# A retention block and two MLPs: the first two loads of weights behind the fourth unit's inputs, and loads planned at 390 bytes a ns

## The chip, the cores and the metric

The kernel runs on one core of a Trainium2 chip. The metric is the device time of one execution in microseconds (us). The kernel before has a median of 909.39 us over 3 runs (909.02 to 910.09). The engines are named as in the profile: PE is TensorE (matmuls), PEld its loads of weights, DVE VectorE, ACT ScalarE, POOL GpSimd, SP SyncE, which issues nearly all DMAs.

## The reference

```python
# retention: 4 batches, 8 heads, 576 positions, 64 dims
scores = (1 / sqrt(64)) * q @ k^T
gamma  = 1 - 2 ** (-5 - head)
ret    = scores * where(i >= j, gamma ** (i - j), 0)
x = (ret @ v)  as [2304 tokens, 512]
# first MLP: w_in 512 x 2048, w_out 2048 x 512
h = maximum(x @ w_in, 0);  x = (h * h) @ w_out
# second MLP: w_a, w_b 512 x 1536, w_out 1536 x 512
return ((x @ w_a) * (x @ w_b)) @ w_out
```

All inputs but q, k and v, which are 32-bit floats, are weights in 64-bit floats.

## The kernel before

**One planner orders everything.** The kernel doesn't issue its instructions as it goes. Each piece of work is a step, added to a list with the engine it uses, its estimated cost and what it depends on (`Plan.add`). `Plan.order` then simulates the engines: working back from the end it gives each step a due time, and going forward it takes, on the engine that is free next, the step that is due first among those that are ready. The result is a fixed order for each engine, and on the chip each engine works through its own strictly in that order. The planner knows loads and stores by the bytes that they move: `dmac` (line 244) costs a transfer of n bytes at n / 260 ns, at least 620 ns. All such transfers go through one queue, issued by SyncE (line 242), again in the planned order.

**Attention** is done in 20 units: for each of 4 batches four pairs of heads over the first 7 chunks of 64 positions, and one unit for the two chunks left of all pairs. A unit loads its queries and keys (tile `qkr`, three buffers) and its values and keys (tile `vr`, three buffers), scales the latter by decays on ScalarE (line 475, tile `tv`), multiplies scores, states and sums on TensorE, masks the scores on VectorE (line 565, tile `pt`), carries states (lines 586 and 587) and writes its product to `xt`, the MLP's input (line 550). The first four units are the head pairs of batch 0. With three buffers, the fourth unit's `qkr` takes the buffer that the first unit has used.

**Weights** come as 64-bit floats, 512 KB for a tile of 128 x 512, into raw buffers (`wraw`: four of their own and two lent from the part of `xt` that is filled last, shown as `xt_68`). `w_load` (lines 321 to 382) turns a raw tile into 32-bit form with integer steps: the magnitude of the high words on ScalarE (line 342, tile `wf`), a clamp, a shift and a sign on VectorE (346, 353, 361), the low words on ScalarE (368, tile `we`) and their addition on VectorE (372). The sum is then split: ScalarE casts its high half into a slot `w` (line 377, shown as the helper's line 233), and VectorE subtracts that from the sum for the low half (line 380, shown as 236). Inputs of the MLPs are split in the same way (`split_x`: a cast at 233 and a subtraction at 236 for each of four tiles `x` of a block of tokens). Each product is then three matmuls: high by high, low by high, high by low.

**The MLPs** run over groups of chunks of the hidden width, each group over five blocks of tokens. The first group (8 chunks of the first MLP) is interleaved with attention: block t is planned when `READY[t]` parts of attention are (two parts to a batch: its four pairs, and its unit for the rest). Weights are loaded in the order of use (`pump`, `todo`), first into 16 slots. When attention is finished, `enter` (line 759) gives its buffers free and puts in their place `yt`, three raw buffers (`raw`) and three further weight slots; a group's result that was stored to memory before that (tile `y`, through `r`) is loaded back into `yt`.

The planner's `extra` argument adds dependencies by hand. Every step's dependencies, also those, hold in the planner's simulation; on the chip, a load waits only for the buffers and data it needs and for its place in SyncE's order. `env` is a small dictionary that attention and the MLPs share.

Of the kernel before, what the change touches and what calls it, by code (L numbers as in the profile page):

```python
# [13 lines left out]
U32 = mybir.dt.uint32  # L14
# [9 lines left out]
NP = H // 2  # L24
# [172 lines left out]
def act(n, psum=False):  # L197
    return 0.833 * n + (110 if psum else 140)

def dve(n):  # L200
    return 1.042 * n + 70

def dve2(n):
    return 0.521 * n + 190

def pool(n):
    return 2.3 * n + 150

@with_exitstack
def tile_retention_two_mlps(  # L210
# [13 lines left out]
    plan = Plan()  # L224
# [7 lines left out]
    def copy(o, i):  # L232
        return lambda e: A.copy(o(), i()) if e == "ACT" else eng[e].tensor_copy(o(), i())  # L233

    def sub(o, a, b):
        return lambda e: eng[e].tensor_sub(o(), a(), b())  # L236
# [4 lines left out]
    def dma(o, i):  # L241
        return lambda e: nc.sync.dma_start(out=o(), in_=i())

    def dmac(bytes_):
        return {"DMA": max(620.0, bytes_ / 260.0)}

    big = ctx.enter_context(tc.tile_pool(name="big", bufs=1))
    dram = ctx.enter_context(tc.tile_pool(name="dram", bufs=1, space=bass.MemoryType.DRAM))
# [10 lines left out]
    def slot(tag):  # L259
        r = rings[tag]  # L260
        i = r[1] % len(r[0])
        r[1] += 1
        plan.renew((tag, i))
        return r[0][i], (tag, i)
# [45 lines left out]
    def raw_slot():  # L310

        if state_["entered"] is None:
            raw, key = slot("wraw")
            return lambda: raw, key, []
        n = state_["loads"]
        state_["loads"] += 1
        key = ("late", n % RAWS)
        plan.renew(key)
        return lambda: raws[n % RAWS], key, [state_["entered"]]

    def w_load(ph, c, j, i):

        w, kw = slot("wf")
        rest, ke = slot("we")
        src = (w1 if ph == 1 else w2)[c, :, j, :]
        parts = [("w", i, 0), ("w", i, 1)]
        ex = [state_["entered"]] if i >= NW0 else []
        wu = w.bitcast(U32)

        raw, kraw, exr = raw_slot()  # L330
        def lo():
            return raw()[:, 0::2]

        def hi():
            return raw()[:, 1::2]

        plan.add(
            dmac(P * 4096),
            dma(raw, lambda: src.bitcast(U32)), w=[kraw], extra=exr,
        )  # L340
        plan.add(
            {"ACT": act(512)}, lambda e: A.activation(w, hi().bitcast(F32), AF.Abs), [kraw], [kw]  # L342
        )
        plan.add(
            {"DVE": dve2(512)},
            lambda e: V.tensor_scalar(  # L346
                out=w, in0=w, scalar1=F64_MIN, scalar2=F64_MAX, op0=ALU.max, op1=ALU.min
            ),
            w=[kw],
        )  # L350
        plan.add(
            {"DVE": dve2(512)},
            lambda e: V.tensor_scalar(  # L353
                out=wu, in0=wu, scalar1=3, scalar2=0x3FFFFFF8,
                op0=ALU.logical_shift_left, op1=ALU.bitwise_and,
            ),
            w=[kw],
        )
        plan.add(
            {"DVE": dve(512)},  # L360
            lambda e: V.scalar_tensor_tensor(  # L361
                out=wu, in0=hi(), scalar=0xC0000000, in1=wu, op0=ALU.bitwise_and, op1=ALU.bitwise_or
            ),
            [kraw], [kw],
        )
        plan.add(
            {"ACT": act(512)},
            lambda e: A.activation(rest, lo(), AF.Copy, scale=LO_ULPS), [kraw], [ke],  # L368
        )
        plan.add(  # L370
            {"DVE": dve(512)},
            lambda e: V._custom_dve(  # L372
                ADD32_U16LIMBS, out=w.bitcast(U16), in0=w.bitcast(U16), in1=rest.bitcast(U16)
            ),
            [ke], [kw],
        )
        plan.add({"ACT": act(512)}, copy(lambda: wslot[i][:, 0, :], lambda: w), [kw], parts[:1], ex)
        plan.add(
            {"DVE": dve(512), "POOL": pool(512)},
            sub(lambda: wslot[i][:, 1, :], lambda: w, lambda: wslot[i][:, 0, :]),  # L380
            [kw, parts[0]], parts[1:], ex,
        )

    def pump():
        while todo:
            i = state_["next"] % state_["n"]
            if i in used.values():
                return
            used[todo[0]] = i
            wt[todo[0]] = i  # L390
            state_["next"] = i + 1
            w_load(*todo.pop(0), i)
# [4 lines left out]
    def attention():  # L397
# [8 lines left out]
        for h in half:  # L406
# [7 lines left out]
                w=[("mask",)],  # L414
            )

        def decays(p):
            plan.add(
                {"DVE": 230},
                lambda e: V.tensor_scalar(  # L420
                    out=md[:, p], in0=mask, scalar1=vt[:, p:p + 1], scalar2=None, op0=ALU.mult
                ),
                [("mask",), ("vt",)], [("md", p)],
            )

        class Unit:
# [13 lines left out]
            def load(self):  # L440
                b, n, m = self.b, len(self.cells), len(self.leave)
                o = 2 * C * LONG * (NP if self.p is None else self.p)
                self.r, self.kr = slot("qkr")
                plan.add(
                    dmac(P * 8 * C * n),
                    dma(lambda: self.r[:, :2 * n * C], lambda: qk[b][:, o:o + 2 * n * C]), w=[self.kr],
                )
                if (b, self.p) == (0, 0):
                    plan.add(
                        {"ACT": 470}, lambda e: A.dma_start(out=vt, in_=vtab), w=[("vt",)], lag=2200  # L450
                    )

                    plan.add(
                        {"ACT": 1500}, lambda e: A.copy(first[:, 1:], first[:, :1]), [("first",)],
                        [("tv", 0)],
                    )
                self.v, self.kv = slot("vr")
                plan.add(
                    dmac(P * 4 * D * (n + m)),
                    dma(lambda: self.v[:, :(n + m) * D], lambda: vk[b][:, o:o + (n + m) * D]),  # L460
                    w=[self.kv],
                )
                if (b, self.p) == (0, 0):
                    plan.add(dmac(P * 4 * C * NP), dma(lambda: gt, lambda: gtab), w=[("gt",)])
                if b == 0 and self.p is not None:
                    decays(self.p)
                self.tv, self.kt = slot("tv")
                for q in self.pairs:
                    js = [i for i, x in enumerate(self.leave) if x[0] == q]
                    vs = [i for i, x in enumerate(self.cells) if x in self.leave and x[0] == q]  # L470
                    to = slice(js[0] * D, (js[-1] + 1) * D)
                    ti = slice(vs[0] * D, (vs[-1] + 1) * D)
                    plan.add(
                        {"ACT": 0.833 * len(js) * D + 250},
                        lambda e, to=to, ti=ti, q=q: A.activation(  # L475
                            self.tv[:, to], self.v[:, ti], AF.Copy, scale=vt[:, NP + q:NP + q + 1]
                        ),
                        [self.kv, ("vt",)], [self.kt],
                    )
# [131 lines left out]

    xs = {}
    y1 = {}
    env = {"done": 0}

    def split_x(gi, t):
        ph = GROUPS[gi][0]
# [269 lines left out]
```

## Time and profile before

| | |
|---|---|
| median of 3 runs | 909.39 us (909.02 to 910.09) |
| profiled execution | 911.62 us, its span 909.9 us |
| PE busy | 893.1 us (98% of the span), 6256 matmuls |
| DVE busy | 490.3 us (54%) |
| ACT busy | 383.2 us (42%) |
| data moved | 66.12 MB, 73 GB/s over the span |
| DMA share in the first six slices of 40 | 0.8, 0.7, 0.8, 0.3, 0.5, 0.3 |

The page divides the span into 40 slices of 22.7 us. TensorE's busy share is 0.6 in the first, 0.8 in the second and 0.9 or more in every other. The DMA engines are busy for the most part in the first three slices, in which attention's inputs and the first weights are loaded. VectorE's share is 0.9 or more in the second and the fourth slice. The trace holds 49 packets of the queue of instructions (q8, 0.80 MB): the engines' programs are themselves read from memory while the kernel runs.

### The profile page before, as it was taken

How to read it: one execution, taken by the hardware profiler on the slowest of the kernel's cores; microseconds unless marked ns; L12 is line 12 of the kernel's file. 1: busy time of each engine (PE TensorE's matmuls, PEld its weight loads, DVE VectorE, ACT ScalarE, POOL GpSimd, SP SyncE). 2: the span in 40 equal slices, each digit the busy share in tenths (PEclk: the TensorE clock that was granted, in tenths of full speed). 3: DMA queues.
4: the chain of work that ended last, by engine and by line, in shares of the span. 5: the costliest groups of instructions: out<-in, count | busy, mean ns of one | idle time of the engine just before them, and what ended most of it. 6: DMA issues, size and time to landing. Idle time of an engine off the chain costs nothing.

```text
span 909.9 us, 14978 instructions
## 1 busy us (share of the span) xinstructions
PE 893.1 (98%) x6256; PEld 755.6 (83%) x6256; DVE 490.3 (54%) x974; ACT 383.2 (42%) x707; POOL 0.7 (0%) x6
## 2 busy tenths in 40 slices
PE   6899999999999999999999999999999999999998
PEld 6787888788898889888888888898888888888888
DVE  6899545721599847965595223289332253323323
ACT  3676334653586435643364223266222132221221
POOL 0000000000000000000000000000000000000000
PEclk9999999999999999999999999999999999999999
DMA  8783532811043300320032000024000000011101
GB/s 276 276 278 124 171 117 71 278 58 58 24 123 110 116 1 24 96 67 1 0 98 89 1 1 1 1 82 142 8 1 1 1 1 1 2 45 47 43 5 70
DMA packets 22100, 66.12 MB, mean 73 GB/s; under 512 B 2448, under 2 KB 3088, under 8 KB 22032
## 3 DMA queue, kind: packets, MB, share of 16 engines
q1 hardware_dynamic: 21888, 65.15, 22.0%
q8 instruction: 49, 0.80, 0.4%
q14 instruction: 19, 0.16, 0.1%
q10 hardware_dynamic: 144, 0.01, 0.0%
HBM read 57.28 MB, written 7.86 MB: 72 GB/s over the span
## 4 chain that ended last, share of the span: by engine, by line
PE 93%; DVE 5%; DMA 1%; ACT 1%; issue 1%; DVEq 0%; ACTq 0%
PE bank L227 93%; DVE wf L372 1%; DVE wf L361 1%; DVE w L236 1%; DVE sa L587 1%; DMA y<-r 0%; DVE pt L565 0%; DMA vt<-vtab 0%; DVE xt L550 0%; DVE wf L346 0%; DVE wf L353 0%; DVE gh L236 0%; ACT r L697 0%; DVE xt L239 0%; ACT tv L475 0%
## 5 line engine op out<-in xcount | busy, mean ns | idle before, releaser
L227 PE MATMUL bank<-x,w 128*128 128x512 f32 (+1 forms) x2400 | 537.2, 369 | 3.4 <-ACT r L697 1.6
L227 PEld LDWEIGHTS bank<-x,w 128*128 128x128 f32 x2400 | 421.3, 189 | 80.8 <-ACT r L697 2.6
L227 PE MATMUL bank<-gh,w 128*128 128x512 f32 (+1 forms) x1680 | 387.1, 369 | 1.2 <-ACT r L233 0.8
L227 PEld LDWEIGHTS bank<-gh,w 128*128 128x128 f32 x1680 | 295.8, 188 | 55.2 <-ACT r L233 1.2
L697 ACT ACTIVATE r<-bank 128x512 f32<-128x512 f32 (+1 forms) x140 | 77.5, 553 | 313.5 <-PE bank L227 310.5
L706 DVE TENSOR_TENSOR g<-bank,r 128x512 f32<-128x512 f32 (+1 forms) x60 | 38.3, 638 | 180.3 <-PE bank L227 179.4
L236 DVE TENSOR_TENSOR gh<-g,gh 128x512 fp32r<-128x512 f32 (+1 forms) x140 | 88.9, 635 | 81.1 <-ACT g L711 56.1
L233 ACT CAST gh<-g 128x512 fp32r<-128x512 f32 (+1 forms) x100 | 57.7, 577 | 110.9 <-DVE g L706 94.8
L236 DVE TENSOR_TENSOR x<-yt,x 128x512 fp32r<-128x512 f32 (+1 forms) x60 | 36.0, 634 | 50.2 <-ACT x L233 50.1
L233 ACT CAST w<-wf 128x512 fp32r<-128x512 f32 x68 | 41.6, 616 | 23.2 <-DVE wf L372 20.6
L236 DVE TENSOR_TENSOR w<-wf,w 128x512 fp32r<-128x512 f32 x68 | 46.5, 686 | 8.8 <-ACT w L233 8.4
L372 DVE CUSTOM_DVE_ANT_0 wf<-wf,we 128x1024 uint16<-128x1024 uint16 x68 | 46.6, 686 | 1.1
L236 DVE TENSOR_TENSOR x<-xt,x 128x512 fp32r<-128x512 f32 (+1 forms) x60 | 37.2, 634 | 12.2 <-ACT x L233 9.2
L702 DVE SCALAR_TENSOR_TENSOR g<-bank,r 128x512 f32<-128x512 f32 (+1 forms) x40 | 25.4, 636 | 30.5 <-ACT r L697 30.2
L368 ACT ACTIVATE we<-raw 128x512 int32<-128x512 uint32 x52 | 34.6, 669 | 14.5 <-DVE wf L372 14.2
L233 ACT CAST x<-xt 128x512 fp32r<-128x512 f32 (+1 forms) x60 | 33.7, 575 | 16.4 <-PE bank L227 15.9
L342 ACT ACTIVATE wf<-raw 128x512 f32<-128x512 f32 x52 | 34.4, 671 | 4.2 <-DMA raw<-w 2.4
L361 DVE SCALAR_TENSOR_TENSOR wf<-raw,wf 128x512 uint32<-128x512 uint32 x52 | 35.3, 686 | 0.2
L233 ACT CAST x<-yt 128x512 fp32r<-128x512 f32 (+1 forms) x60 | 33.4, 576 | 4.9 <-PE bank L227 4.0
L346 DVE TENSOR_SCALAR wf<-wf 128x512 f32<-128x512 f32 x68 | 28.1, 421 | 5.2 <-ACT wf L342 4.6
L239 DVE TENSOR_TENSOR yt<-bank,yt 128x512 f32<-128x512 f32 (+1 forms) x40 | 23.3, 630 | 11.3 <-PE bank L227 11.3
L353 DVE TENSOR_SCALAR wf<-wf 128x512 uint32<-128x512 uint32 x68 | 28.1, 421 | 0.3
(42 smaller groups left out, 365.9 us busy)
## 6 DMA issues: line engine op xcount, KB each, us to landing
raw<-w SPq DMA_DIRECT2D x52, 512.0 KB, 3.7
vr<-vk SPq DMA_DIRECT2D x16, 448.0 KB, 4.6
qkr<-qk SPq DMA_DIRECT2D x16, 448.0 KB, 5.0
wraw<-w SPq DMA_DIRECT2D x12, 512.0 KB, 6.5
out<-xt SPq DMA_DIRECT2D x16, 256.0 KB, 2.1
y<-r SPq DMA_DIRECT2D x12, 256.0 KB, 3.0
yt<-y SPq DMA_DIRECT2D x3, 1024.0 KB, 8.4
qkr<-qk SPq DMA_DIRECT2D x4, 512.0 KB, 4.9
```

What stands on the lines that cost most here:

```text
L227: T.matmul(o, l, r, start=start, stop=stop, skip_group_check=True)
L233: return lambda e: A.copy(o(), i()) if e == "ACT" else eng[e].tensor_copy(o(), i())
L236: return lambda e: eng[e].tensor_sub(o(), a(), b())
L342: {"ACT": act(512)}, lambda e: A.activation(w, hi().bitcast(F32), AF.Abs), [kraw], [kw]
L346: lambda e: V.tensor_scalar(out=w, in0=w, scalar1=F64_MIN, scalar2=F64_MAX, op0=ALU.max, op1=ALU.min),
L353: lambda e: V.tensor_scalar(out=wu, in0=wu, scalar1=3, scalar2=0x3FFFFFF8, op0=ALU.logical_shift_left, op1=ALU.bitwise_and,),
L361: lambda e: V.scalar_tensor_tensor(out=wu, in0=hi(), scalar=0xC0000000, in1=wu, op0=ALU.bitwise_and, op1=ALU.bitwise_or),
L368: lambda e: A.activation(rest, lo(), AF.Copy, scale=LO_ULPS), [kraw], [ke],
L372: lambda e: V._custom_dve(ADD32_U16LIMBS, out=w.bitcast(U16), in0=w.bitcast(U16), in1=rest.bitcast(U16)),
L697: lambda e, o=o: A.activation(r[:, :n], o[:, :n], fn), [ko], [kr],
L702: V.scalar_tensor_tensor(out=g[:, :n], in0=o[:, :n], scalar=0.0, in1=r[:, :n], op0=ALU.max, op1=ALU.mult)
L706: V.tensor_mul(g[:, :n], o[:, :n], r[:, :n])
```

## The change

The planner's cost of a transfer goes from bytes / 260 to bytes / 390 ns. And while `env["hold"]` holds a step, every load of a raw weight gets it as a further dependency. The step is the load of queries and keys of the unit (0, NP - 1), the fourth unit; the number `len(plan.steps)` is the one that the load is about to get. Nothing sets `hold` back, so that it stands in the dependencies of the later loads of weights too, where it has long been fulfilled.

```diff
     def dmac(bytes_):
-        return {"DMA": max(620.0, bytes_ / 260.0)}
+        return {"DMA": max(620.0, bytes_ / 390.0)}
...
         plan.add(
             dmac(P * 4096),
-            dma(raw, lambda: src.bitcast(U32)), w=[kraw], extra=exr,
+            dma(raw, lambda: src.bitcast(U32)), w=[kraw], extra=exr + env["hold"],
         )
...
                 self.r, self.kr = slot("qkr")
+                if (b, self.p) == (0, NP - 1):
+                    env["hold"] = [len(plan.steps)]
                 plan.add(
                     dmac(P * 8 * C * n),
                     dma(lambda: self.r[:, :2 * n * C], lambda: qk[b][:, o:o + 2 * n * C]), w=[self.kr],
                 )
...
-    env = {"done": 0}
+
+    env = {"done": 0, "hold": []}
```

What this does to the order shows best at three places. The first is SyncE's queue at the start, as the difference of the two orders: `wraw` and `xt_68` are raw weights, `qkr` and `vr` the inputs of attention's units; the six loads of the first three units and the table `gt` stand ahead of this piece.

```order
-L242 DMA wraw_125<-w 128x1024
-L242 DMA wraw_127<-w 128x1024
 L242 DMA qkr_113<-qk 128x896
 L242 DMA vr_116<-vk 128x896
+L242 DMA wraw_125<-w 128x1024
 L242 DMA vr_117<-vk 128x768
 L242 DMA qkr_114<-qk 128x1024
-L242 DMA wraw_126<-w 128x1024
+L242 DMA wraw_127<-w 128x1024
 L242 DMA qkr_115<-qk 128x896
 L242 DMA vr_118<-vk 128x896
+L242 DMA wraw_126<-w 128x1024
```

The two weights that stood ahead of the fourth unit's `qkr_113` stand behind it now, the first one place after its `vr_116`, and the third weight moves two places back; `xt_68` follows in both orders, and in the new one `wraw_128` stands right behind it, where two loads of the seventh unit came first.

The second place is ScalarE and VectorE at the first block of the MLP, where `x_84` to `x_87` are the split halves of its inputs. On ScalarE, as the difference of the two orders:

```order
 L342 ACTIVATE wf_79<-wraw_126 128x512
 L368 ACTIVATE we_83<-wraw_126 128x512
-L475 ACTIVATE tv_120<-vr_118,vt 128x448
-L233 CAST w_95<-wf_79 128x512
+L342 ACTIVATE wf_78<-xt_68 128x512
+L342 ACTIVATE wf_81<-wraw_128 128x512
 L233 CAST x_84<-xt_65 128x512
 L233 CAST x_85<-xt_65 128x512
 L233 CAST x_86<-xt_65 128x512
 L233 CAST x_87<-xt_65 128x512
```

The conversions of the fourth and the fifth raw weight (`xt_68` and `wraw_128`) now stand ahead of the four casts of x; the scaling of the sixth unit's values and the cast of the third weight have moved behind them.

On VectorE before, at the same place, the four subtractions of x in their surroundings:

```order
L372 ISA wf_79<-wf_79,we_83 128x1024
L550 TENSOR_TENSOR xt_65<-bank_76,gt 128x4x64
L550 TENSOR_TENSOR xt_66<-bank_76,gt 128x4x64
L565 TENSOR_TENSOR pt_122<-bank_74,md 128x448
L236 TENSOR_TENSOR w_95<-wf_79,w_95 128x512
L236 TENSOR_TENSOR x_84<-xt_65,x_84 128x512
...
L236 TENSOR_TENSOR x_87<-xt_65,x_87 128x512
L586 COPY sa_124<-bank_75 128x64
```

And on VectorE in the changed order (its lines are two or three further down):

```order
L552 TENSOR_TENSOR xt_65<-bank_76,gt 128x4x64
...
L236 TENSOR_TENSOR x_84<-xt_65,x_84 128x512
...
L236 TENSOR_TENSOR x_87<-xt_65,x_87 128x512
L236 TENSOR_TENSOR w_96<-wf_80,w_96 128x512
L372 ISA wf_79<-wf_79,we_83 128x1024
...
L567 TENSOR_TENSOR pt_122<-bank_74,md 128x448
L236 TENSOR_TENSOR w_95<-wf_79,w_95 128x512
...
L552 TENSOR_TENSOR xt_66<-bank_76,gt 128x4x64
```

Five steps that came before the subtractions of x come behind them now: the subtractions for `w_95` and `w_96`, the addition for `wf_79`, the mask `pt_122` and the product into `xt_66`.

The third place is ScalarE at the change of phase (`enter`), where `raw` are the first weights after it and `r` the results that are emptied from the banks. Before:

```order
L233 COPY r_90<-bank_71 128x512
L342 ACTIVATE wf_78<-raw_2119 128x512
L368 ACTIVATE we_82<-raw_2119 128x512
L233 COPY r_91<-bank_72 128x512
L342 ACTIVATE wf_79<-raw_2120 128x512
L233 CAST w_2122<-wf_78 128x512
L233 COPY r_90<-bank_73 128x512
```

In the changed order:

```order
L233 COPY r_90<-bank_71 128x512
L342 ACTIVATE wf_78<-raw_2118 128x512
L368 ACTIVATE we_82<-raw_2118 128x512
L342 ACTIVATE wf_79<-raw_2119 128x512
L368 ACTIVATE we_83<-raw_2119 128x512
L342 ACTIVATE wf_80<-raw_2120 128x512
L233 COPY r_90<-bank_73 128x512
L233 CAST w_2121<-wf_78 128x512
```

The raw buffers' numbers are one lower. The copy out of `bank_72` has left ScalarE (it stands on VectorE now), and the conversion of the third raw weight stands ahead of the copy out of `bank_73`.

## Rows read from the trace of the kernel before

**Rows 1.** Timeline of TensorE, 12.5 to 17.1 us: start, busy, instructions [idle before <-releaser]

```profile
14.75 1.45 PE L227 MATMUL bank<-pt,vr 64*64 64x64 f32 x25 [1.88 <-issue]
...
16.97 0.36 PE L227 MATMUL bank<-qkr 64*64 64x64 f32 x1
```

**Rows 2.** Waits of TensorE: who waits <- for whom: us, times, longest

```profile
PE bank L227 <- DVE w L236: 0.4, 1, 0.4
```

**Rows 3.** Stretches: length, busy PE, PEld, DVE, ACT, POOL (instructions), clock, DMA share, GB/s

```profile
0.00:5.00 5.00, 0.00 (x0) 0.00 (x0) 0.44 (x4) 1.92 (x3) 0.67 (x6) 1.00 0.61 199
5.00:10.00 5.00, 4.72 (x122) 4.72 (x124) 3.16 (x12) 0.89 (x2) 0.00 (x0) 1.00 1.03 413
20.00:25.00 5.00, 3.83 (x126) 3.69 (x128) 4.96 (x16) 3.04 (x9) 0.00 (x0) 1.00 0.94 309
25.00:32.00 7.00, 4.87 (x130) 4.12 (x129) 6.83 (x15) 4.02 (x9) 0.00 (x0) 1.00 1.02 387
70.00:85.00 15.00, 15.00 (x275) 11.95 (x273) 15.00 (x37) 9.94 (x18) 0.00 (x0) 1.00 0.41 135
```

**Rows 4.** Timeline of VectorE around the first subtractions of x, and its last wait

```profile
29.11 0.75 DVE L550 TENSOR_TENSOR xt<-bank,gt 128x256 f32<-128x256 f32 x2
29.78 0.61 DVE L565 TENSOR_TENSOR pt<-bank,md 128x448 f32<-128x448 f32 x1
30.91 2.49 DVE L236 TENSOR_TENSOR x<-xt,x 128x512 fp32r<-128x512 f32 x4
...
57.31 0.69 DVE L236 TENSOR_TENSOR w<-wf,w 128x512 fp32r<-128x512 f32 x1 [0.56 <-ACT w L233]
```

**Rows 5.** Waits of VectorE, 32 to 58 us

```profile
DVE sa L586 <- PE bank L227: 1.4, 2, 0.9
DVE w L236 <- ACT w L233: 0.8, 2, 0.6
DVE wf L346 <- ACT wf L342: 0.8, 1, 0.8
DVE gh L236 <- ACT g L711: 0.4, 1, 0.4
```

**Rows 6.** Timeline of SyncE: the issue of some loads

```profile
0.80 0.38 SPq L242 DMA_DIRECT2D vr<-vk  x1
...
4.55 0.82 SPq L242 DMA_DIRECT2D wraw<-w  x2
11.45 0.33 SPq L242 DMA_DIRECT2D qkr<-qk  x1
...
17.62 0.33 SPq L242 DMA_DIRECT2D qkr<-qk  x1
```

**Rows 7.** DMA queues, 12.0 to 12.2 us, then 12.2 to 12.4: packets, MB, share

```profile
q1 hardware_dynamic: 18, 0.05, 63.5%
...
q8 instruction: 1, 0.02, 32.9%
q1 hardware_dynamic: 9, 0.01, 17.1%
```

**Rows 8.** Loads from issue to landing, 0 to 100 us: tile qkr, then tile w

```profile
DMA to landing us min/median/max: 3.9/5.2/9.8
...
DMA to landing us min/median/max: 4.4/6.8/11.0
```

**Rows 9.** Timeline of ScalarE: the first conversion of a weight, the first casts of x

```profile
11.81 0.67 ACT L342 ACTIVATE wf<-wraw 128x512 f32<-128x512 f32 x1 [1.03 <-DMA wraw<-w]
...
29.75 2.18 ACT L233 CAST x<-xt 128x512 fp32r<-128x512 f32 x4
```

**Rows 10.** Change of phase: SyncE's load of the third raw weight; TensorE's two waits

```profile
153.30 0.43 SPq L242 DMA_DIRECT2D raw<-w  x1
...
161.22 0.96 PE L227 MATMUL bank<-gh,w 128*128 128x512 f32 x3 [0.82 <-ACT r L233]
...
163.08 1.20 PE L227 MATMUL bank<-x,w 128*128 128x512 f32 x4 [0.90 <-ACT r L697]
```

## The prediction

> **What bounds the kernel now.** I read the busy shares first (TensorE has work over 893.1 of 909.9 us, on the page), then TensorE's waits, then the busy time by stretches, and last the queues of the first 90 us in order of time. TensorE's work is the same in both kernels, so only its stops count, 909.9 - 893.1 = 16.8 us, the wait for the first input and the tail behind the last matmul among them. What can move are the stops of the first 90 us and two at the change of phase near 161 us. At 12.9 us TensorE stands still for 1.88 us with "issue" as the reason, that is, for nothing that the profile shows as a wait [rows 1]. And at 85 us it waits for VectorE's low half of a weight [rows 2]. VectorE is busy 15.00 of 15.00 us from 70 to 85 [rows 3], and its last wait before that ends at 57.31 us [rows 4]; those between 32 and 58 us are four kinds, 3.4 us together [rows 5]. So from 57 to 85 us VectorE sets the pace, and TensorE arrives there as early as VectorE lets it. That is the yardstick for all that happens at the start: a lead of TensorE at 31 us is worth what VectorE can keep of it.
>
> **What the change does not do.** In the kernel before, the fourth unit's queries and keys leave SyncE at 11.45 us, long after the two weight loads at 4.55 [rows 6], because they need the buffer that the first unit's sums set free. In the changed order the same matmuls release them. The weights did not take their place in the queue; what they did was to fill the DMA engines up to 12.3 us.
>
> **Part 1, the stop at 12.9 us.** It falls inside one step (25 of its matmuls follow at 14.75 [rows 1]), so no operand is what it waits for. The queue of instruction packets handles its first packet in the window 12.2 to 12.4, just as the data queue falls from a share of 63.5% to 17.1% [rows 7]. By bytes: 0.995 MB in the first 5 us (5.00 x 199) and 413 GB/s after it [rows 3] put the end of the first seven loads (2.88 MB) at 9.6 us and of the two weights (3.93 MB) at 12.1. I read it so: the instructions waited behind the weights. Without these the packet can go at about 10, some 2.2 us sooner, and the stop of 1.88 us goes.
>
> The Trainium skill, DMA: Bandwidth & Descriptors, section "Queues, rings and completion order", says that each DMA engine serves its queues in turn, a packet at a time; an instruction packet would then wait for one packet of data and not for a megabyte. By that rule the stop is not the weights' doing, and it stays; the second rival gives the time of this case. The rows at 12.2 us speak against it, but they are one event.
>
> What is late next, once the stop is gone: the fourth unit's queries and keys. The shortest landing of such a load is 3.9 us [rows 8], which makes 15.35 for the scores that stood at 16.97 [rows 1]: 1.6 us earlier. The fifth unit's load is issued when the second unit's sums end; those took 2.9 us from 14.75 to 17.62 [rows 1, 6] and end by 15.8 when they go on at 12.9, so it is at least 1.8 us earlier at issue, though now behind a weight.
>
> **Part 2, the later weights.** The first weight leaves SyncE at about 12.3 instead of 4.55. What decides is ScalarE's order before the first x casts: it now converts two more raw weights there, the last of them the fifth load (wraw_128). From the fourth unit's queries and keys to that load SyncE issues eleven transfers: five weights of 0.524 MB, queries and keys of 0.459, 0.524 and 0.459, values and keys of 0.459, 0.393 and 0.459, together 5.37 MB. Bytes begin some 1.8 us after an issue (0.995 MB by 5.0 us at 413 GB/s means a start near 2.6, and the first issue is at 0.80 [rows 3, 6]), so here at 13.3. At the 387 GB/s of 25 to 32 us [rows 3] the last byte is there at 27.2. A landing shows 1.0 us after its last byte (first weight: 10.8 by bytes, and ScalarE starts on it at 11.81 [rows 9]), so 28.2; one conversion of 0.67 [rows 9], and the x casts start at 28.9 instead of 29.75 [rows 9], 0.85 earlier. At 413 GB/s it is 28.0 (the fifth unit's last product on VectorE, at 29.11 before [rows 4] and up to 1.6 earlier now, allows that): 1.75 earlier. At the 309 GB/s of 20 to 25 us [rows 3] it is 32.4, or 2.65 later. I take 387, the row of the stretch that is most like it, with a queue that is never empty.
>
> **Part 3, what VectorE keeps.** With casts at 28.9 VectorE's first x subtraction is at 29.5 instead of 30.91 [rows 4], 1.4 earlier. But five steps that stood ahead of it now stand behind: two weight subtractions and one limb addition, each as long as an x subtraction (2.49 / 4 = 0.62), one mask of scores (0.61) and one product on 256 columns (0.75 / 2 = 0.37), 2.8 us [rows 4]. VectorE is therefore 1.4 us behind at that place although TensorE is ahead. Afterwards it can only make up what it idled before, 1.4 + 0.8 + 0.8 + 0.4 = 3.4 us [rows 5]. The bounds at 57 us are 1.4 us later (nothing made up) and 2.0 earlier (all of it). The waits for TensorE (1.4) shrink because TensorE comes 1.4 us sooner, and ScalarE's (2.0) hang mostly on casts that are queued behind TensorE's results, so both lean to the upper half: I take three quarters, 2.6 made up, 1.2 us earlier. VectorE has no idle time from there to 85 us that could give or take, so TensorE gains 1.2 us at its wait at 85 us.
>
> **Part 4, the change of phase at 150 us.** The third load of the second set of weights now stands right behind the second, two stores of y come behind it, the evacuation of the third bank moves from ScalarE to VectorE, and ScalarE converts the third raw weight before it empties the fourth bank. Before, TensorE waits 0.82 and 0.90 us here, to 161.22 and 163.08 [rows 10]. The third load issues at 153.30 + 0.43 [rows 10] and lands 6.8 us later (median of the queued weight loads; 4.4 and 11.0 are the ends [rows 8]), at 160.5; a conversion and a copy of some 0.65 each, and TensorE goes on at 161.8, 0.6 late. The second wait ends after one cast and one more evacuation, near 162.9, 0.2 early, and what counts is the second: 0.2 gained. The ends are 1.7 gained (both waits gone) and, with a landing after 11.0 us, 2.9 lost.
>
> The rest of TensorE's order differs in neighbours that swap and in numbers of tiles. I cost it at nothing: the late weights are prepared under matmuls that run without a stop from 165 us to the last block, and that cover is missing only at 85 and 161 us, which are counted.
>
> **Sum.** The profiled execution takes 911.62 us, its span of 909.9 and 1.7 around it: 911.62 - 1.2 - 0.2 = 910.2. The median of the runs shown, 909.39, is 2.2 below it, so the forecast is 909.39 - 1.4 = 908.0.
>
> **Rivals.**
> 1. Slower: the fifth weight load becomes the wait. ScalarE works in order, so the x casts and all behind them stand behind that one conversion. If the load lands after 29.1 us (29.75 less the conversion), no lead is left; at 309 GB/s VectorE's first x subtraction is 2.05 late with 2.8 us of work behind it, 4.85 together, of which 2.6 are made up: 2.25 later, less the 0.2, 911.4. For it: the 309 GB/s were measured on just such mixed loads. Against: 413 and 387 on either side.
> 2. The stop stays, and the change doesn't do what it says. The fourth unit starts at 16.97, the x casts stay at 29.75, VectorE has 2.8 us of work behind them and makes up 2.6, the change of phase gives 0.2: 909.4, no change.
> 3. All is kept: VectorE makes up its whole 3.4 us (2.0 gained) and half of the two stops at 161 us goes (0.9): 906.5. For it: the lead of TensorE is 1.4 to 2 us by the first two parts. Against: the 2.8 us that VectorE carries.
>
> **How the numbers follow.** Forecast 0.42, the slower rival 0.20, the stop stays 0.20, all is kept 0.18. A measurement of this kernel can tell 0.2%, or 1.8 us, from no change, and 908.0 lies just inside it. Of the forecast I put 0.17 beyond 907.6 and 0.25 within, of the slower rival 0.17 beyond 911.2 and 0.03 within, of the stop that stays 0.16 within and 0.04 slower (the third load's late landing falls here). Faster is 0.17 and the third rival's 0.18, 0.35; within are 0.25, 0.03 and 0.16, 0.44; slower 0.17 and 0.04, 0.21. The range goes from 905.8, a little below the third rival, to 911.6, just past the first; the forecast's own is 906.8 to 909.3.
>
> **What would show it.** Right: no stop with "issue" near 13 us, an instruction packet near 10 to 11, the fourth unit's scores at 15 to 15.5, x casts at 28 to 29.5, VectorE without idle time from some 50 us on. Wrong: a stop inside the same step; ScalarE idle for a weight's DMA ahead of the x casts, past 29.1; VectorE's waits between 32 and 58 us as long as before; more than 1.7 us of stops near 161 us.

## The result and the profile after

| | before | after |
|---|---|---|
| median | 909.64 us (4 runs) | 919.93 us (4 runs, 918.76 to 920.34) |
| ratio | | 1.0108, 95% interval 1.0096 to 1.012 |
| profiled execution, its span | 911.62, 909.9 us | 919.74, 918.0 us |
| PE busy | 893.1 us | 894.7 us |

The change makes the kernel 1.1% slower, some 10.3 us; 908.0 was forecast, 911.6 the upper end of the range. The timeline of TensorE after, with the stops of the start and the one at the change of phase (columns as in [rows 1]):

```profile
15.86 0.86 PE L227 MATMUL bank<-qkr 64*64 64x64 f32 x22 [1.07 <-DMA qkr<-qk]
19.00 1.03 PE L227 MATMUL bank<-tv,vr 64*64 64x64 f32 x28 [0.76 <-ACT tv L477]
21.69 1.15 PE L227 MATMUL bank<-qkr 64*64 64x64 f32 x32 [1.66 <-DMA qkr<-qk]
25.02 0.86 PE L227 MATMUL bank<-qkr 64*64 64x64 f32 x22 [1.73 <-DMA qkr<-qk]
31.07 3.37 PE L227 MATMUL bank<-x,w 128*128 128x512 f32 x12 [1.16 <-ACT x L233]
36.29 4.59 PE L227 MATMUL bank<-x,w 128*128 128x512 f32 x12 [1.86 <-ACT r L700]
57.22 0.49 PE L227 MATMUL bank<-gh,w 128*128 128x512 f32 x1 [1.44 <-ACT w L233]
...
168.61 0.96 PE L227 MATMUL bank<-gh,w 128*128 128x512 f32 x3 [3.55 <-ACT r L233]
```

The stop with "issue" of 1.88 us [rows 1] is gone. In its place stand three waits for queries and keys, a weight that is late at 57 us, and one long stop at 168 us where there were two short ones [rows 10].

**A second trace of each kernel.** Both kernels were run and profiled once more, because single executions of one kernel differ by as much as the terms in question. The kernel before then took 908.86 us (its span 907.1, 2.8 us below that of the first trace). The granted clock shows most of the difference. The stretches of the first trace of before, columns as in [rows 3]:

```profile
15.00:20.00 5.00, 4.97 (x130) 4.83 (x125) 2.53 (x8) 1.05 (x3) 0.00 (x0) 0.66 0.52 136
...
30.00:35.00 5.00, 4.09 (x11) 2.93 (x12) 5.00 (x12) 3.63 (x7) 0.00 (x0) 0.71 1.02 392
```

The same stretches of its second trace:

```profile
15.00:20.00 5.00, 4.27 (x134) 3.92 (x132) 5.00 (x15) 1.75 (x3) 0.00 (x0) 1.00 0.98 345
...
30.00:35.00 5.00, 3.82 (x16) 2.76 (x16) 5.00 (x13) 4.35 (x9) 0.00 (x0) 1.00 1.01 404
```

So I read the loss against the second trace. The ruler is the moments at which ScalarE empties bank 7 (line 697 or 700, `r<-bank`): the first group's chunks come in the same order in all these kernels. The table, worked out from ScalarE's timelines, gives how many us later than in the second trace of before each comes, and the same for the span.

```
                 1st    2nd    5th   16th   span
second before    33.2   37.0   59.3  142.7  907.1
first before     +2.6   +2.6   +2.6   +2.6   +2.8
after            +2.4   +4.0   +7.9   +7.3  +10.9
after, again     +3.7   +3.7   +7.6   +7.0  +11.0
hold_only        +1.7   +1.7   +1.9   +2.4   +2.4
rate_only        +4.8   +4.7   +4.7   +4.5   +8.3
both_late260     +4.1   +5.6   +9.3   +8.7   +9.9
vr_lag           +1.1   +1.1   +1.4   +1.9   +6.6
vr_lag_late260   +1.8   +1.8   +2.1   +2.7   +5.4
rate_late        +0.6   +0.6   +0.6   +0.6   +3.3
lat_short        +6.4   +8.1   +5.4   +5.2   +7.3
one_early260     +0.6   +0.6   +0.6   +0.5   +0.3
one_late160      +0.8   +0.8   +0.8   +0.7   +2.8
one_late200      +0.6   +0.6   +0.6   +0.5   +0.7
```

The two traces of the changed kernel agree: about 7 us are lost before 145 us, 3.9 of them between the second and the fifth emptying (0.6 come back by the 16th), and 3.6 to 4 at the change of phase. Of the 2.4 and 3.7 us at the first emptying hold_only has 1.7 too. The two places that the hold alone doesn't have are shown now.

**The first place: ScalarE stands in front of values that have not landed.** ScalarE's waits from 36 to 72 us, after (who waits <- for whom: us, times, longest):

```profile
ACT tv L477 <- DMA vr<-vk: 5.4, 3, 2.9
ACT w L233 <- DVE wf L372: 2.9, 3, 1.5
```

In both traces of before, `tv` waits for no load in this stretch, for there it stands behind the emptying of the bank. The fourth emptying in the second trace of before, on ScalarE:

```profile
51.81 0.60 ACT L697 ACTIVATE r<-bank 128x512 f32<-128x512 f32 x1 [1.24 <-PE bank L227]
52.30 0.34 ACT L475 ACTIVATE tv<-vr,vt 128x64 f32<-128x64 f32 x1
```

After, `tv` comes first. The longest of the three waits, in ScalarE's timeline after:

```profile
52.77 0.67 ACT L342 ACTIVATE wf<-xt 128x512 f32<-128x512 f32 x1 [0.19 <-DVE w L236]
56.31 0.35 ACT L477 ACTIVATE tv<-vr,vt 128x64 f32<-128x64 f32 x1 [2.87 <-DMA vr<-vk]
56.56 0.60 ACT L233 CAST w<-wf 128x512 fp32r<-128x512 f32 x1
57.07 0.66 ACT L368 ACTIVATE we<-wraw 128x512 int32<-128x512 uint32 x1
57.64 0.58 ACT L700 ACTIVATE r<-bank 128x512 f32<-128x512 f32 x1
```

The chain of waits around it (start, us, what):

```profile
51.18 5.05 DMA vr<-vk
...
56.31 0.35 ACT tv L477
56.66 0.52 ACT w L233
...
57.19 0.70 DVE w L236
...
57.94 2.08 PE bank L227 x8
```

The load of 393,216 bytes takes 5.05 us from issue to landing. At 390 bytes a ns the planner has it there after 1.0 + 2.1 = 3.1 us and puts `tv` where the values would then be. At 260 it has them there after 1.5 + 2.1 = 3.6 us, and the same load took 4.3 us in the second trace of before: too early as well, but there it had landed at 51.51, before ScalarE came to `tv`. On the chip ScalarE stops, and the cast of a weight behind `tv`, VectorE's subtraction and TensorE's matmul stop with it. TensorE's stops between the second emptying and 72 us are 2.2 us together (1.44, 0.23 and 0.5; none in before); the rest of the 3.3 us that stay lost shows as no stop, and where it goes is open.

**The second place: a store behind two loads.** SyncE now issues the second and the third raw weight together and then the next stores of y. The chain at the change of phase, after:

```profile
160.11 0.60 ACT r L233
...
160.73 7.15 DMA y<-r
...
167.97 0.47 ACT r L233
...
168.46 0.62 ACT w L233
```

This is the second of four stores. The same one in the second trace of before, issued at 153.46:

```profile
DMA to landing us min/median/max: 3.0/3.0/3.0
```

The store of y takes 7.15 us instead of 3.0. Until it is through, the buffer `r` isn't free, the copy out of the fourth bank waits, and TensorE, which goes on when that bank is empty, with it. The chain names the wait that came last; ScalarE's timeline shows two more of nearly the same end, for the second and the third raw weight, behind whose conversions the copy is queued:

```profile
165.88 0.66 ACT L342 ACTIVATE wf<-raw 128x512 f32<-128x512 f32 x1 [3.52 <-DMA raw<-w]
166.45 0.65 ACT L368 ACTIVATE we<-raw 128x512 int32<-128x512 uint32 x1
167.14 0.67 ACT L342 ACTIVATE wf<-raw 128x512 f32<-128x512 f32 x1
167.97 0.58 ACT L233 COPY r<-bank 128x512 f32<-128x512 f32 x1 [0.16 <-DMA y<-r]
```

The two loads, issued at 158.66 and 159.13 us, from issue to landing:

```profile
DMA to landing us min/median/max: 7.2/7.6/8.0
```

They land at 165.86 and 167.12, the store at 167.87. The third weight's conversion starts as soon as it has landed, at 167.14, and ends 0.16 us before the copy: without the store's wait the copy would have gone only that much earlier. So two loads and a store that share the queue all land late, and the copy waits for the loads by its place on ScalarE and for the store by its buffer; by these times taking away one of them would leave the others, which no run tries one by one. Behind this stop the clock falls. Two stretches after:

```profile
35.00:40.00 5.00, 3.71 (x10) 2.89 (x11) 4.77 (x14) 3.94 (x8) 0.00 (x0) 0.67 0.63 216
169.00:174.00 5.00, 4.94 (x15) 3.61 (x14) 4.04 (x7) 2.68 (x6) 0.00 (x0) 0.66 0.93 322
```

A mean of 0.66 over 5 us, with single microseconds at 0.50 and at 1.00, is 1.2 GHz instead of 2.4 for a good part of the stretch and costs 5 x (1 - 0.66) = 1.7 us. At the change of phase stops of 3.55 instead of 0.53 + 1.05 in the second trace of before are 2.0 us, the clock 1.7: 3.7 together, as in the table (10.9 - 7.3). The low stretch at 169 us is in both traces of the changed kernel, the one at 36 us only in the first; the second has one between 15 and 30 us instead (0.77 on average) and comes to the first emptying 1.3 us later.

### The profile page after: what moved, and what is told of

Its sections match the earlier page's. It is cut to its first block, busy times and chain, and to the rows that moved or that the text cites. A ratio compares the mean times of both kernels' runs of the same rounds, so it can differ in the third digit from the quotient of the medians.

```text
span 918.0 us, 14993 instructions
## 1 busy us (share of the span) xinstructions
PE 894.7 (97%) x6256; PEld 755.6 (82%) x6256; DVE 491.2 (54%) x976; ACT 383.4 (42%) x705; POOL 0.7 (0%) x6
## 4 chain that ended last, share of the span: by engine, by line
PE 92%; DMA 3%; DVE 3%; ACT 1%; issue 1%; ACTq 0%
PE bank L227 92%; DMA vr<-vk 1%; DMA qkr<-qk 1%; DMA y<-r 1%; DVE wf L361 0%; DMA vt<-vtab 0%; DVE wf L372 0%; DVE w L236 0%; ACT r L700 0%; DVE sa L589 0%; DVE wf L346 0%; DVE wf L353 0%; DVE pt L567 0%; ACT w L233 0%; DVE xt L552 0%
## 5 line engine op out<-in xcount | busy, mean ns | idle before, releaser
L233 ACT CAST w<-wf 128x512 fp32r<-128x512 f32 x68 | 41.5, 614 | 17.0 <-DVE wf L372 14.7
L342 ACT ACTIVATE wf<-raw 128x512 f32<-128x512 f32 x52 | 34.5, 672 | 14.8 <-DMA raw<-w 12.5
```

## The experiments

**Which half of the change.** hold_only leaves `dmac` at 260 and keeps the hold; rate_only sets 390 and has no hold.

```diff
# hold_only, against the changed kernel
-        return {"DMA": max(620.0, bytes_ / 390.0)}
+        return {"DMA": max(620.0, bytes_ / 260.0)}
# rate_only, against the kernel before
-        return {"DMA": max(620.0, bytes_ / 260.0)}
+        return {"DMA": max(620.0, bytes_ / 390.0)}
```

> The hold alone: transfers stay planned at 260 bytes a ns. SyncE's start is that of the changed kernel (no weight ahead of the fourth unit's inputs), the change of phase that of the kernel before, and ScalarE casts x before it converts the third, fourth and fifth weight. Theory A (the rate of 390 costs the time, at the start by the conversions that it puts ahead of the x casts, at the change of phase by the third weight that it puts right behind the second): 907 to 910 us, no stop with issue near 13 us, x casts ahead of 30.4. Theory B (the hold costs it, since the first weights come 8 us later and the DMA engines stand idle from 10 to 13.5 us): 912 to 915, with the waits for queries and keys (4.5 us) and for a weight near 57 us as in the changed kernel.

> The rate of 390 alone: no hold. Four weights now stand ahead of the fourth unit's inputs. Theory A: 917 us or more, with both losses of the changed kernel. Theory B: 913 us, the loss at the change of phase alone (some 3.5 us). On the stop near 13 us: if instruction packets wait for the data that were queued before them, four weights (2.1 MB at 413 GB/s) end at 14.7 us instead of 12.1 and the stop lasts to some 17.3 us (4.4 instead of 1.88); if they are served in turn, the stop is 1.9 as before or gone.

hold_only took 910.96 us, ratio 1.0009 (1.0001 to 1.0018), rate_only 920.13, ratio 1.011 (1.009 to 1.0131). The rate is the cause; the hold costs 0.2% at most. With the hold alone no `tv` waits between 36 and 72 us, and the change of phase is that of before:

```profile
161.12 0.96 PE L227 MATMUL bank<-gh,w 128*128 128x512 f32 x3 [0.89 <-ACT r L233]
162.74 3.01 PE L227 MATMUL bank<-x,w 128*128 128x512 f32 x12 [0.66 <-ACT r L700]
```

With the rate alone ScalarE waits for values from 8 to 72 us, and the stop at the change of phase is there again:

```profile
ACT tv L475 <- DMA vr<-vk: 12.7, 7, 3.2
```

```profile
166.03 0.97 PE L227 MATMUL bank<-gh,w 128*128 128x512 f32 x3 [3.65 <-ACT r L233]
```

rate_only loses its start earlier than the changed kernel (4.8 us at the first emptying); four weights stand ahead of the inputs there, which I take for the reason, though no run separates it. Between the second and the fifth emptying it loses nothing (+4.7 at both), although `tv` waits there too, 3.5 us in three. So the first place as it stands in the changed kernel comes from the rate and the hold together: the hold spares the loss at the start, and ScalarE's order further on takes the saving back.

**How many weights ahead of the inputs.** one_early260 plans at 260 and lets the first weight go ahead.

```diff
# one_early260, against hold_only
-            dma(raw, lambda: src.bitcast(U32)), w=[kraw], extra=exr + env["hold"],
+            dma(raw, lambda: src.bitcast(U32)), w=[kraw], extra=exr + (env["hold"] if len(todo) < 67 else []),
```

> Transfers at 260; the hold for all weights but the first, so that one weight instead of two (before) or none (changed) stands ahead of the fourth unit's inputs. If the first instruction packet waits for the data queued before it: the data end at 10.8 us instead of 12.1, the packet comes then, TensorE goes on at some 13.5 and the stop at 12.9 is 0.6 instead of 1.88. If not, 1.88 or none. Time by theory A 907 to 909.5 us, by theory B (late weights cost) between before and hold alone, 910 to 912.

909.29 us, ratio 0.9997 (0.9988 to 1.0006): no difference. There is no stop at 12.9 us; 0.6 had been expected. The first packet of the instruction queue comes at 9.8 to 10.6 us with no weight early (changed kernel and hold_only), at 10.8 to 11.2 with one (this kernel and the three further on that begin so), at 12.2 to 12.8 with two (before twice and rate_late), and at 12.4 to 12.6 with four (rate_only). So the fourfold case fell short: I had expected the packet at 14.7 us and a stop of 4.4, and it was 1.00. There the data queue goes on beside the packet. Rows of rate_only, 12 to 13 and 13 to 14 us (packets, MB, share):

```profile
q1 hardware_dynamic: 98, 0.35, 88.8%
q8 instruction: 1, 0.02, 5.9%
...
q1 hardware_dynamic: 106, 0.41, 103.7%
```

The packet thus does not wait for all data in the queue. The Trainium skill, DMA: Bandwidth & Descriptors, section "Queues, rings and completion order", has the engines serve their queues in turn; the row of rate_only agrees with that and the rows with none, one and two weights do not obviously. What the packet waits for stays open. What hangs on it is plainer. Six traces have the stop, 0.19 to 1.88 us long: before twice, rate_only, rate_late, lat_short and one_late160. In each of them 222 matmuls stand ahead of it, and TensorE goes on 2.0 to 2.7 us behind the packet, at 14.75 to 15.00 us with two and four weights early and at 13.43 and 13.67 with one, however long it has stood. In the second trace of before it had stood for only 0.38 us by then:

```profile
14.76 0.97 PE L227 MATMUL bank<-pt,vr 64*64 64x64 f32 x25 [0.38 <-issue]
```

**The first place by itself.** vr_lag changes one number in the changed kernel: when the planner believes values of batches 1 to 3 to be there.

```diff
                     dma(lambda: self.v[:, :(n + m) * D], lambda: vk[b][:, o:o + (n + m) * D]),
-                    w=[self.kv],
+                    w=[self.kv], lag=4400 if b else None,
```

> The changed kernel with one number more: the planner believes that the loads of values (vr) of batches 1 to 3 are there 4.4 us after their transfer, not 2.1. SyncE's order stays (but for one place at the sixth unit); on ScalarE the scalings tv move behind the emptying of the MLP's bank and its squares. Theory A2 (the start's loss arises between 36 and 67 us because ScalarE stands in a tv for values that have not landed, 5.4 us in three waits, with casts of weights behind it): the three waits shrink to below 2 us, the third to sixth emptying of the bank come within 1.5 us of before's (47.0, 54.4, 61.9, 69.3), and the time is 919.9 less some 3.5 = 916 us, with the 3.5 us of the change of phase left. Rival (weights stand ahead of the inputs in the queue, so TensorE waits for the inputs wherever tv stands): 919 to 921, and TensorE waits for tv or qkr instead.

917.29 us, ratio 1.0085 (1.0063 to 1.0108). The loss between the first and the fifth emptying is gone (+1.1 and +1.4 instead of +2.4 and +7.9), and so are the waits. ScalarE's from 36 to 80 us:

```profile
ACT w L233 <- DVE wf L372: 8.1, 7, 2.2
ACT r L700 <- PE bank L227: 2.3, 4, 1.0
```

SyncE's order is the same but for one place, so it was not the queue that made TensorE wait, but where ScalarE stands when the values are late. By the medians this is worth 2.6 us, by the traces some 5.4 at the 16th emptying (1.65 of them the low clock at 36 us); the profiled execution has the lowest of the four times (915.42), so I go by the medians. What is left is the change of phase. It loses 4.6 us here (+1.9 to +6.6), 0.6 to 1.0 more than in the changed kernel: the stop is as long (3.60), and the granted clock is 0.54 from 163 to 170 us.

**The second place by itself.** both_late260 is the changed kernel with 260 behind the change of phase; rate_late the kernel before with 390 there; vr_lag_late260 has both remedies.

```diff
# both_late260 and, on top of vr_lag, vr_lag_late260
-        return {"DMA": max(620.0, bytes_ / 390.0)}
+        return {"DMA": max(620.0, bytes_ / (390.0 if state_["entered"] is None else 260.0))}
# rate_late, against the kernel before
-        return {"DMA": max(620.0, bytes_ / 260.0)}
+        return {"DMA": max(620.0, bytes_ / (260.0 if state_["entered"] is None else 390.0))}
```

> The changed kernel up to the change of phase (hold, 390), but transfers planned behind it at 260. Should the 3.55 us stop at 168.6 us and the low clock behind it come from the third raw weight's place right behind the second: 919.9 less 1.9 (stops) and 1.65 (clock) = 916.4 us, and the stops there 1.7 as before. Rival: they come from the late arrival of attention's last unit, whatever the order: 919 to 920.

> The kernel before, with transfers behind the change of phase planned at 390: the third raw weight right behind the second, as in the changed kernel, but attention as before. If the order there costs what it seems to (a stop of 3.5 us instead of 0.8 and 0.9, and 3 us at half the clock behind it): 909.6 + 1.9 + 1.6 = 913.1 us. If it needs attention's late arrival too: 910.

> Both remedies: values of batches 1 to 3 believed there 4.4 us after their transfer, and 260 behind the change of phase; hold and 390 ahead of it stay. If the two places are all that the rate of 390 costs: 919.9 - 3.5 - 2.5 = 914 or less, down to 911. If tv is not the cause: 917 to 919.

both_late260 took 919.06 us (ratio 1.0098), hardly less; that was nearer to the rival. Its trace tells why: it recovers at the change of phase (+8.7 before it, +9.9 at the end, where the changed kernel has +7.3 and +10.9), but it came there 1.4 us later. Its two stops:

```profile
168.04 0.96 PE L227 MATMUL bank<-gh,w 128*128 128x512 f32 x3 [1.58 <-ACT r L233]
170.18 3.02 PE L227 MATMUL bank<-x,w 128*128 128x512 f32 x12 [1.18 <-ACT r L700]
```

rate_late, which has attention untouched, took 912.12 us, ratio 1.0021 (1.0009 to 1.0033): the order at the change of phase costs 2 us by itself, without a late arrival (2.7 in its trace, 1.7 of them a clock of 0.66 from 161 to 166 us). In its trace ScalarE stands in front of the second raw weight:

```profile
157.84 0.67 ACT L342 ACTIVATE wf<-raw 128x512 f32<-128x512 f32 x1 [1.98 <-DMA raw<-w]
```

vr_lag_late260 took 914.02 us, ratio 1.0046 (1.0028 to 1.0065). The two remedies together take back 5.9 of the 10.3 us, where they took 2.6 and 0.9 apart; with some 1 us of spread in each median I don't read more into the sum. At the change of phase it still loses 2.7 us (+2.7 to +5.4). Its third raw weight stands one store earlier than in before, and its stops are 1.38 and 1.18 us, 1.0 more than there; the other 1.7 are the clock:

```profile
164.00:169.00 5.00, 4.70 (x15) 3.79 (x15) 4.31 (x9) 3.94 (x8) 0.00 (x0) 0.66 0.83 257
```

both_late260, with longer stops in the same order, has no such stretch. That is nearly all of the 3.0 us by which its span exceeds hold_only's (912.5 and 909.5).

**Bandwidth, or the moment of landing.** lat_short is the kernel before, with the planner's time from the end of a transfer to its data shortened.

```diff
-    LAT = {"PE": 200, "DMA": 2100, "ACT": 160, "DVE": 150}
+    LAT = {"PE": 200, "DMA": 1428, "ACT": 160, "DVE": 150}
```

> The kernel before at 260 bytes a ns, but with the planner's time from the end of a transfer to its data at 1428 instead of 2100 ns: a weight of 512 KB is believed there after 2016 + 1428 = 3444 ns, as with 390 (1344 + 2100). No hold. If what counts is when the planner believes data to be there: tv ahead of the bank's emptying as in the changed kernel, ScalarE waits for values between 30 and 72 us, and 912 to 914 us, with the change of phase as before. If what counts is how many transfers it believes the queue to manage: 909 to 910.

915.03 us, ratio 1.0052 (1.0033 to 1.007): too early a landing costs time also where the bandwidth is the old one. It does so elsewhere than expected. Some 2 us are lost at the change of phase (+5.2 to +7.3), where no loss had been expected. Between 36 and 80 us `tv` waits 0.9 us only; ahead of that the conversions of weights stand in front of the casts of x. TensorE's waits from 5 to 36 us:

```profile
PE bank L227 <- ACT tv L475: 6.1, 2, 5.2
PE bank L227 <- ACT x L233: 5.6, 1, 5.6
```

**A better version was not found.** one_late160 and one_late200 go the other way behind the change of phase, on top of one_early260.

```diff
-        return {"DMA": max(620.0, bytes_ / 260.0)}
+        return {"DMA": max(620.0, bytes_ / (260.0 if state_["entered"] is None else 160.0))}   # or 200.0
```

> The opposite of the change at the change of phase: one weight ahead of the fourth unit's inputs (as one_early260), 260 in attention, and 160 bytes a ns behind it, which puts all four stores of y ahead of the third raw weight and the copies of the banks ahead of the second weight's conversion. If the copies of the banks wait there for their buffers' stores behind raw weights, the two stops of 0.6 and 0.7 us shrink below 0.4 together and the time is some 1 us below one_early260's 909.3: 908 to 908.8. If the second weight becomes late instead, a stop for a cast or a weight takes their place: 909 to 911.

> The same with 200 bytes a ns behind the change of phase: the stores keep their places, the conversion of the second weight goes behind the copy of the fourth bank. Stops as in one_early260 or 0.5 us less: 908.7 to 909.5 us.

one_late160 took 911.79 us, ratio 1.0019 (1.0008 to 1.0031), a miss: with all stores first the stop moves to the emptying of bank 7 and lasts longer.

```profile
161.53 4.26 PE L227 MATMUL bank<-x,w 128*128 128x512 f32 x12 [2.07 <-ACT r L700]
```

one_late200 took 909.68 us, ratio 1.0001 (0.9992 to 1.001). None of the kernels that were run beats the one before.

**Both kernels again,** unchanged, for the second traces:

> The kernel before itself once more, for a second trace and the spread of its time: no difference in the time; the stop with issue near 12.9 us again at 1.5 to 2 us, the first instruction packet again behind the two weights, at 12 to 12.5 us.

> The changed kernel itself once more, for a second trace: 919.9 us within 1; the waits of ScalarE for values between 36 and 67 us (5.4 us in three) and the stop of 3.5 us at 168 us again. Whether the two stretches at half the clock (near 36 and 171 us) are there again tells if they belong to the order or to the execution.

909.45 us, ratio 0.9999 (0.9989 to 1.0008), and 920.77, ratio 1.0128 (1.011 to 1.0146). The stop at 12.9 us was 0.38 and not 1.5 to 2 us; the waits for values were 5.5 us in three again, the stop at 168 us 3.93.

## Why the prediction was wrong, step by step

**What bounds the kernel:** that VectorE sets the pace to 85 us held for before. In the changed kernel it didn't: VectorE waited 4.9 us for ScalarE's casts between 30 and 72 us. (By the page of before its share is 0.9 or more in the third and the fourth slice, and 0.8 in the second.)

**Part 1, the stop at 12.9 us:** right in what happens. The first instruction packet came at 9.8 to 10.0 us (about 10 was said), the stop went, the fourth unit's scores stood at 15.86 (15.35 was said). The packet, after, 9.8 to 10.0 us (packets, MB, share):

```profile
q8 instruction: 1, 0.02, 33.5%
q1 hardware_dynamic: 8, 0.00, 5.7%
```

What was wrong is its worth: in the second trace of before the stop is 0.38 us, and the kernels without it (one_early260, hold_only) are no faster.

**Part 2, the later weights:** the casts of x came at 30.41, not 28.9, with ScalarE waiting 0.52 us for the fifth weight just ahead, which landed at 29.8 and not at 28.2. VectorE's first subtraction of x came at 31.13, where 29.5 was said, so 1.6 us of the lead were missing at this point. The first rival's mechanism was there, with a smaller delay than it reckoned with.

**Part 3, what VectorE keeps:** the step that failed. I let VectorE make up 2.6 of the 3.4 us of its waits because ScalarE's casts "are queued behind TensorE's results". I had compared ScalarE's order as far as the casts of x and not behind them, where the scalings `tv` now stand ahead of the bank's emptying. 1.2 us gained were forecast at 85 us; it was a loss of 4.7 against the trace used (7.3 against the other), by the eighth emptying.

**Part 4, the change of phase:** the path was the one that was said, the third weight's landing, its conversion, the copy of the fourth bank, but it was mis-sized. The load took 8.0 us to land instead of 6.8 (8.5 in the second trace), and it was issued 0.7 us later, counted from the 16th emptying. The second weight and the store of y, which I had not looked at, landed at 165.9 and 167.9, each some 7.2 us after its issue. 0.2 gained were forecast, with 2.9 lost as one end; it was 3.7, 2.0 of it the stop and 1.7 the clock, which I had not priced.

**The rest, at nothing:** right from 175 us on; the lag of 11 us behind the change of phase is still that of the span.

**The rivals:** none of them looked at ScalarE behind the casts of x. The slower one (911.4) had the right idea, an engine that works in order in front of a transfer, but for one load of weights only.

## What to carry to other kernels

In a plan that is fixed beforehand for engines that work in order, the cost of a transfer says above all when its data are believed to be there. Believed too early (3.1 us against 5.05), the consumer can be put ahead of work that is ready, and everything behind it waits. The belief at 260 was too early too (3.6 against 4.3) and did no harm, because the consumer's turn came after the landing; so after a change of such a cost compare each engine's order for steps that read a load, to the end of the phase, and look for stores whose buffers are awaited behind loads in one queue. And take two traces before pricing a stop of a microsecond.

## What the runs showed of the hardware

A stop with "issue" at the start falls ahead of the same matmul in six traces and ends 2.0 to 2.7 us after the first packet of the instruction queue, whatever its length (0.19 to 1.88 us). A stretch at half the clock, which cost 1.7 us, followed the stop of 3.5 to 3.9 us at the change of phase in both traces of the changed kernel. It followed stops of 1.38 and 1.18 us in vr_lag_late260 and didn't follow 1.58 and 1.18 in both_late260; others, at 15, 32 or 36 us, were there in one execution and not in the next of the same kernel. A store of 256 KB took 3.0 to 3.3 us from issue to landing where the last transfer issued before it was a single load of 512 KB (before twice, hold_only), and 7.1 to 7.5 behind two (the changed kernel twice, rate_only, vr_lag).
